# Eight more rows of the second batch's first stage computed before the steady loop, the last reads of the first batch's way back on other queues, and the first token group's sums by halves

## The chip, the cores and the metric

The kernel runs on one core of a Trainium2 chip. A core has a TensorE for matrix products (PE), a VectorE (DVE), a ScalarE (ACT), a GpSimd (POOL) and a SyncE (SP) that issues transfers; transfers run on 16 DMA engines. Metric: the device time of one execution in microseconds (us), the median over the runs shown.

## The reference

Eight batches of 3008 tokens by 256 channels go through a Fourier filter along the tokens, and the result goes token by token through a two-layer network of 2048 hidden units:

```python
X = np.fft.rfft(x, axis=1)
Y = X * (filt_r + 1j * filt_i)[None]
y = np.fft.irfft(Y, n=x.shape[1], axis=1)
h = y.reshape(B * S, D) @ w_in
out = (h - np.tanh(h)) @ w_out
```

x and the filters are float32; the weights arrive as 64-bit floats and are turned into float32 on the chip.

## The kernel before

3008 tokens are taken as 64 times 47. The forward transform has a **first stage** (for each residue r of 0 to 23 one product of a 128-row factor with 128 rows of x, called "row r" here, result into the DRAM buffer `ct1[b]`), a **middle** (products over the residues, the filter, products back, result into `ct2[b]`), and a **last** stage that reads `ct2[b]` for a group of 4 residues and leaves the group's tokens, transposed, in the tile `ut`. Six groups of 448 or 512 tokens make a batch. Each group then goes through four units U of the network: `up` (x, y, z, o banks), `shrink` (h minus tanh h, on ACT and DVE), `down` (accumulates the output). A unit counter U runs over 192 units; unit U issues its `up`, the `shrink` of U - 1 and the `down` of U - 2, interleaved by hand (the schedule is manual: every engine's queue holds its instructions in the order in which the program issues them).

**The prologue** (pools `pro` and `ps0`) does the whole transform of batch 0 up to `ct2[0]`, slot by slot: seven slots g, each with `across`, `there0`, `filtered` and a way back (`back0`, for the last slot `back`) whose results are copied by ACT to tiles e1 and stored into `ct2[0]` (trace name ct<-e). The stores of slots 0 to 2 are issued by POOL, 3 and 4 by SP, 5 by ACT, 6 half by ACT and half by SP. When slots 0 to 4 are stored, `rest(0, 25, ...)` (line 1129) reads 25 rows of each of four blocks into the tile `e2` of the first token group; when 5 and 6 are stored, a second `rest` reads the other 7 rows of each (trace name e<-ct). Both are four reads, issued by SP. Then SP issues the first loads of `first(2)` (see below), PE does rows 0 to 7 of batch 1 (`first1`, line 1227; four ACT copies, four stores on SP, line 1234) and 8 warming products (`warmer(8)`, line 1081) whose results are not used.

**Around it** the weights are converted from 64 bits by a chain of steps, one on ACT (line 181) and six or seven on DVE (lines 183 to 201), and combined by sums on DVE (lines 229, 232, 238). `convert(100)` issues what is left of the first five conversion jobs; the other eleven (`late`) are spread over the units U up to 5 by `converting(n)`. Their raw data is loaded by POOL (line 175).

**Then** `last(0)` (line 595 on PE, tile pu) makes the first group's tokens: 64 small products into two banks, "even" and "odd", an ACT copy of odd (line 601), a DVE sum and a DVE difference (lines 605, 606) into `ut`. Four further warming products (line 1374) fill PE until `ut` is there, and U = 0 starts (line 719, tile x).

**First stages in the loop.** `first(2, z2, [(1, c) for c in range(2, NX)])` is a generator of ten steps: rows 8 to 23 of batch 1 (four steps of four rows) and all of batch 2 (six). A step (lines 308 to 313, trace name pf) is four products into two banks, two ACT copies into the one tile a1, and a store by ACT. The list `due` says at which position 20c + 5u + k (group c, unit u of the group, place k of 0 to 4 in the unit) the next step is issued: ten positions from 4 on, 3 apart.

Of the kernel before, what the change touches and what calls it, by code (L numbers as in the profile page):

```python
# [9 lines left out]
F32 = mybir.dt.float32  # L10
# [11 lines left out]
SG = 5  # L22
# [95 lines left out]
def kernel(  # L118
# [27 lines left out]
    def dram(t, off, dims):  # L146
        return bass.AP(tensor=t, offset=off, ap=[list(d) for d in dims])
# [112 lines left out]
            for u in dict(after).get(k, ()):  # L260
                yield from sums(u)

    def load_x(t, b, r, n):

        nc.sync.dma_start(t[0:64, 0:n, :], dram(x.tensor, (b * SEQ + r) * DM,
                                                [[NR * DM, 64], [1, n * DM]]))
        lo = 1 if r == 0 else 0
        if lo:
            nc.sync.dma_start(t[64:128, 0, :], dram(x.tensor, b * SEQ * DM,
                                                    [[NR * DM, 64], [1, DM]]))  # L270
        nc.sync.dma_start(t[64:128, lo:n, :], dram(x.tensor, (b * SEQ + NR - r - lo) * DM,
                                                   [[NR * DM, 64], [-DM, n - lo], [1, DM]]))
        return t

    rows = slice(0, 64), slice(64, 128)
# [302 lines left out]
    def widths(c):  # L578

        return [128 if r else 64 for r in order(c)]  # L580
# [3 lines left out]
    def last(i, z, held=False):  # L584

        b, c = groups[i]
        n = sum(widths(c))
        e2, gt = e2s.pop(i)
        ut = dn.tile([128, 2, CH * 128], F32, tag="ut", bufs=2, name="ut")
        banks = z("pu", [128, 2, CH, 64])  # L590
        for h in range(2):
            for j, r in enumerate(order(c)):
                for bank, half in zip(banks, rows):
                    for m, part in enumerate(rows):
                        nc.tensor.matmul(bank[part, h, j],  # L595
                                         e2[half, r - CH * c, h * 128 + 64 * m:h * 128 + 64 * m + 64],
                                         gt[half, r - CH * c], start=True, stop=True)
        even, odd = banks
        for k in (1, 0) if held else (1,):
            t = tr.tile([128, 2, CH, 64], F32, tag="e1", bufs=2, name=("even", "odd")[k])  # L600
            ACT.copy(t, banks[k])
            even, odd = (even, t) if k else (t, odd)
        u4 = ut.rearrange("p h (j n) -> p h j n", n=128)
        m = sum(w == 128 for w in widths(c))
        V.tensor_add(u4[:, :, :, 0:64], even, odd)
        V.tensor_sub(u4[:, :, 0:m, 127:63:-1], even[:, :, 0:m], odd[:, :, 0:m])
        w = n // 2
        if i == 0:
            uts[i] = (ut, None, w)
            yield  # L610
            return
# [420 lines left out]
    with tc.tile_pool(name="tr", bufs=2) as tr, tc.manual_schedule():  # L1032
# [16 lines left out]
        with tc.tile_pool(name="pro", bufs=1) as pro, \  # L1049
# [169 lines left out]

            first0(2)  # L1220

            def first1(x1):

                for r in range(0, 8, 2):
                    pf = z0("pf", [128, 2, DM])
                    for k in range(2):
                        nc.tensor.matmul(pf[:, k], f0[:, r + k], x1[:, r + k],
                                         start=True, stop=True)
# [4 lines left out]
                    ACT.copy(a1, pf)  # L1233
                    nc.sync.dma_start(
                        dram(ct1[1], r * DM, [[NH * DM, 128], [1, 2 * DM]]), a1)
                    yield

            a2 = {0: across(0)}
            convert(5)
# [19 lines left out]
            for g in range(last_g + 1):  # L1259
                if g == 2:  # L1260
                    x1 = load_x(big([128, 8, DM], F32, "x1"), 1, 0, 8)
                if g + 2 <= last_g:
                    a2[g + 2] = across(g + 2)
                    if g + 2 < last_g:
                        fts[g + 2] = filters_of(g + 2)
                        if g == 1:
                            fts[last_g] = filters_of(last_g)
                    else:
                        turned_in(fts[last_g])
                if g == 3:  # L1270
# [37 lines left out]
            next(late)  # L1308
            warmer(8)

        with tc.tile_pool(name="dn", bufs=2) as dn, \
                tc.tile_pool(name="ps", bufs=1, space=bass.MemoryType.PSUM) as ps:
# [57 lines left out]
            for _ in last(0, z2):  # L1370
                pass
            warm = psl([128, 256], "o3")
            for _ in range(4):
                nc.tensor.matmul(warm[0:KM], mats[:, 3 * KM:4 * KM], mats[:, 3 * KM:3 * KM + 256],
                                 start=True, stop=True)
# [147 lines left out]
```

## Time and profile before

| what | us |
|---|---|
| median of 3 runs | 2543.22 (2541.65 to 2544.98) |
| profiled execution, its time | 2542.18 |
| profiled execution, its span | 2540.3 |
| PE busy | 2522.6 |
| DVE busy | 1935.6 |
| the first token group's products (pu) start | 76.05 |
| U = 0 starts | 79.77 |

A row of the timeline is: start in us from the span's start, length in us, engine, line, operation, written tile, read tiles, shapes and count, and in brackets how long the engine had been idle and what ended that. A fp32 product counts twice in the rows. SPq, ACTq and POOL rows with DMA_DIRECT2D are the issues of transfers. In the chain of waits a row is start, length, and what the time went to. A row of the stretches is the stretch, its length, busy time and count of PE, PEld, DVE, ACT, POOL, the granted clock, the DMA share and GB/s.

### The profile page before, as it was taken

Reading aid. Unit: us, or ns where it says so; the run is one execution under the profiler, and the core shown is the slowest. Engines: PE = TensorE matmul, PEld = TensorE weight load, DVE = VectorE, ACT = ScalarE, POOL = GpSimd, SP = SyncE. Lnnn points to the kernel's source line nnn. Section 1 sums busy time; section 2 is a strip of 40 time slices with the busy share of each in tenths; the row PEclk is TensorE's granted clock in tenths of the full one; section 3 lists DMA queues with packets and bytes.
Section 4 is the critical chain, followed back from the end, with each engine's and each line's share of the span. In section 5 each row is a group of like instructions: output and inputs, shape, how many; then the busy total and the mean of one; then the engine's idle time right before and its main releaser. Section 6 shows DMA issues by size and latency. Waiting matters only on the chain.

```text
span 2540.3 us, 44575 instructions
## 1 busy us (share of the span) xinstructions
PE 2522.6 (99%) x17072; PEld 2173.1 (86%) x17072; DVE 1935.6 (76%) x2270; ACT 1694.2 (67%) x2551; POOL 1532.0 (60%) x1112
## 2 busy tenths in 40 slices
PE   9999999999999999999999999999999999999998
PEld 8678889888898888988888888898889888898887
DVE  6888877988678876888669886698866888555555
ACT  4666666667666766676667666666666666666665
POOL 5255665667556765676656665666655666455552
PEclk9999999999999999999999999999999999999999
DMA  9854224422343323342334322343123322110110
GB/s 245 261 150 117 65 54 100 112 65 53 86 108 91 82 69 89 80 112 59 80 87 105 87 56 72 96 111 89 36 72 84 92 66 53 26 31 19 25 22 19
DMA packets 333664, 211.37 MB, mean 83 GB/s; under 512 B 231645, under 2 KB 305531, under 8 KB 329793
## 3 DMA queue, kind: packets, MB, share of 16 engines
q1 hardware_dynamic: 319091, 184.93, 29.8%
q0 software_dynamic: 11120, 16.16, 2.3%
q10 hardware_dynamic: 3230, 7.34, 0.9%
q8 instruction: 136, 2.23, 0.4%
q14 instruction: 87, 0.71, 0.1%
HBM read 127.81 MB, written 83.39 MB: 83 GB/s over the span
## 4 chain that ended last, share of the span: by engine, by line
PE 96%; DVE 2%; DMA 1%; issue 0%; POOL 0%; ACT 0%; ACTq 0%; SPq 0%; POOLq 0%; DVEq 0%
PE o L821 44%; PE x L648 25%; PE z L648 12%; PE y L648 6%; PE pm L415 2%; PE pu L595 2%; PE pm L351 1%; PE o L883 1%; PE pf L308 1%; DMA filt<-in_filt_r_dram 1%; DMA x<-in_x_dram 0%; DMA ct<-e 0%; PE o L719 0%; PE x L719 0%; PE z L719 0%
## 5 line engine op out<-in xcount | busy, mean ns | idle before, releaser
L821 PE MATMUL o<-t,wd 128*128 128x256 f32 (+1 forms) x3008 | 762.7, 376 | 0.0
L619 POOL TENSOR_TENSOR t<-h 128x512 f32<-128x512 f32 (+1 forms) x184 | 303.6, 1650 | 707.3 <-DVE h L771 642.2
L771 DVE TENSOR_TENSOR h<-h,y 128x1024 f32<-128x1024 f32 (+1 forms) x384 | 571.0, 1487 | 156.4 <-ACT y L767 156.4
L821 PEld LDWEIGHTS o<-t,wd 128*128 128x128 f32 x3008 | 568.8, 190 | 84.5 <-POOL o L853 15.1
L648 PE MATMUL x<-tu,wu 128*128 128x256 f32 (+1 forms) x2256 | 571.4, 376 | 0.0
L821 PE MATMUL o<-h,wd 128*128 128x256 f32 (+1 forms) x2256 | 569.9, 375 | 0.2 <-DVE h L771 0.2
L648 PEld LDWEIGHTS x<-tu,wu 128*128 128x128 f32 x2256 | 427.4, 190 | 53.8 <-issue 3.9
L821 PEld LDWEIGHTS o<-h,wd 128*128 128x128 f32 x2256 | 428.3, 190 | 50.9 <-issue 0.8
L654 ACT COPY s<-x 128x512 f32<-128x512 f32 (+1 forms) x188 | 109.3, 581 | 517.4 <-PE x L648 517.3
L764 ACT ACTIVATE y<-y 128x1024 f32<-128x1024 f32 (+1 forms) x384 | 399.5, 1040 | 12.1
L767 ACT ACTIVATE y<-y 128x1024 f32<-128x1024 f32 (+1 forms) x384 | 399.8, 1041 | 4.6
L761 ACT ACTIVATE y<-h 128x1024 f32<-128x1024 f32 (+1 forms) x384 | 400.6, 1043 | 2.5 <-DVE h L697 1.7
L622 POOL TENSOR_TENSOR t<-h,t 128x512 f32<-128x512 f32 (+1 forms) x184 | 338.3, 1838 | 0.0
L620 POOL TENSOR_TENSOR t<-h,t 128x512 f32<-128x512 f32 (+1 forms) x184 | 310.5, 1688 | 14.4
L621 POOL TENSOR_TENSOR t<-h 128x512 f32<-128x512 f32 (+1 forms) x184 | 276.9, 1505 | 0.0
L654 ACT COPY u<-x 128x512 f32<-128x512 f32 (+1 forms) x376 | 214.1, 569 | 72.9 <-PE x L648 69.6
L697 DVE COPY h<-x 128x512 f32<-128x512 f32 (+1 forms) x188 | 127.6, 679 | 129.1 <-PE x L648 128.9
L689 DVE TENSOR_TENSOR h<-z,u 128x512 f32<-128x512 f32 (+1 forms) x188 | 127.2, 677 | 88.9 <-ACT u L654 88.5
L648 PE MATMUL x<-ut,wu 128*128 128x256 f32 (+1 forms) x752 | 194.0, 380 | 0.2 <-DVE h L697 0.2
L648 PE MATMUL z<-tu,wu 128*128 128x256 f32 (+1 forms) x752 | 190.2, 375 | 1.4 <-DVE h L705 1.4
L648 PE MATMUL y<-ut,wu 128*128 128x256 f32 (+1 forms) x752 | 190.1, 375 | 0.0
L648 PE MATMUL z<-ut,wu 128*128 128x256 f32 (+1 forms) x752 | 190.0, 375 | 0.0
(215 smaller groups left out, 2933.5 us busy)
## 6 DMA issues: line engine op xcount, KB each, us to landing
ft<-filt SPq DMA_DIRECT2D x28, 1024.0 KB
ct<-nn SPq DMA_DIRECT2D x56, 512.0 KB
e<-ct SPq DMA_DIRECT2D x47, 512.0 KB
a<-ct SPq DMA_DIRECT2D x112, 192.0 KB
out_dram<-ot SPq DMA_DIRECT2D x1248, 16.0 KB
x_sb<-in_x_dram SPq DMA_DIRECT2D x110, 128.0 KB
ct<-a SPq DMA_DIRECT2D x60, 128.0 KB
ct<-x_sb SPq DMA_DIRECT2D x60, 128.0 KB
```

The source lines that it names most:

```text
L619: by.tensor_sub(t[0], b[0][1], b[0][0])
L620: by.tensor_sub(t[1], b[1][1], t[0])
L621: by.tensor_sub(t[2], b[1][1], b[0][1])
L622: by.tensor_sub(t[3], b[1][0], t[1])
L648: nc.tensor.matmul(bank[:, k], wu[:, q - 1, (2 * u + k) * 128:(2 * u + k + 1) * 128], rhs[q - 1], start=(first and k == 0), stop=True, ski ...
L654: ACT.copy(t, X)
L697: V.tensor_copy(h[:, 2, :, 0:w], X)
L761: ACT.activation(y[k], ht[k], AF.Arctan, scale=TURN)
L764: ACT.activation(y[k], y[k], AF.Tanh, scale=BEND)
L767: ACT.activation(y[k], y[k], AF.Square, scale=SCALE, accum_out=y_sums[:, 2 * U + k // 2:2 * U + k // 2 + 1])
L771: V.tensor_mul(ht[k], ht[k], y[k])
L821: nc.tensor.matmul(product(q), wd[:, q - 1, (2 * u + k) * 128: (2 * u + k + 1) * 128], rhs[q - 1][:, k], start=(u == 0 and k == 0 and q == ...
```

## The change

- `load_x` takes a queue. In slot 5 of the prologue POOL issues two more loads: rows 8 to 15 of batch 1 (`x1b`, 1 MB in all), ahead of two raw weight loads.
- The first `rest` (25 rows) is issued by POOL instead of SP. The second is issued alternately by SP and ACT.
- `convert(100)` and rows 0 to 7 (`first1(x1, 0, ...)`) now stand ahead of the second `rest`; rows 8 to 15 (`first1(x1b, 8, ...)`) behind it. `first1` is an ordinary function now; its stores are issued by POOL, two of 4 KB a partition instead of four of 2 KB, for each eight rows. The tiles of rows 8 to 15 are two of the `raw` buffers.
- `warmer(8)` becomes `warmer(2)`, the four warming products after pu become two.
- `first(2, ...)` has eight steps instead of ten, and `due` eight positions from 4 on, 3.75 apart.
- For the first token group the copy, the sum and the difference of `last` are made for each half of the channels.

```diff
-    def load_x(t, b, r, n):
+    def load_x(t, b, r, n, queue=nc.sync):
...
+        if i == 0:
+            t = tr.tile([128, 2, CH, 64], F32, tag="e1", bufs=2, name="odd")
+            for h in range(2):
+                ACT.copy(t[:, h], odd[:, h])
+                V.tensor_add(u4[:, h, :, 0:64], even[:, h], t[:, h])
+                V.tensor_sub(u4[:, h, 0:m, 127:63:-1], even[:, h, 0:m], t[:, h, 0:m])
+            uts[i] = (ut, None, n // 2)
+            yield
+            return
...
-            def first1(x1):
-
-                for r in range(0, 8, 2):
+            def first1(x1, at, tiles):
+
+                for r in range(at, at + 8, 2):
...
                     if r % 4 == 0:
-                        two = (tr.tile([128, 2, 2, DM], F32, tag="a1", bufs=1, name="a1") if r else
-                               buffer("xy").rearrange("p (m n) c -> p m n c", m=2))
-                    a1 = two[:, r // 2 % 2]
-                    ACT.copy(a1, pf)
-                    nc.sync.dma_start(
-                        dram(ct1[1], r * DM, [[NH * DM, 128], [1, 2 * DM]]), a1)
-                    yield
+                        two = tiles.pop(0)()
+                    ACT.copy(two[:, r // 2 % 2], pf)
+                    if r % 4:
+                        G.dma_start(dram(ct1[1], (r - 2) * DM, [[NH * DM, 128], [1, 4 * DM]]),
+                                    two.rearrange("p m n c -> p (m n c)"))
...
                 if g == last_g - 1:
+                    x1b = load_x(big([128, 8, DM], F32, "x1b"), 1, 8, 8, G)
                     ahead += [begun(tiles1, job, queue=G) for job in jobs[7:9]]
...
-            rest(0, SG * (last_g - 1), [nc.sync])
+            rest(0, SG * (last_g - 1), [G])
             way_back()
-            rest(SG * (last_g - 1), NA - SG * (last_g - 1), [nc.sync])
-            fs = first(2, z2, [(1, c) for c in range(2, NX)])
+            convert(100)
+            first1(x1, 0, [lambda: buffer("xy").rearrange("p (m n) c -> p m n c", m=2),
+                           lambda: tr.tile([128, 2, 2, DM], F32, tag="a1", bufs=1, name="a1")])
+            rest(SG * (last_g - 1), NA - SG * (last_g - 1), [nc.sync, ACT])
+            fs = first(2, z2, [(1, c) for c in range(4, NX)])
             next(fs)
-            convert(100)
-            for _ in first1(x1):
-                pass
+            first1(x1b, 8, [raw_tile, raw_tile])
...
-            warmer(8)
+            warmer(2)
...
-            for _ in range(4):
+            for _ in range(2):
                 nc.tensor.matmul(warm[0:KM], mats[:, 3 * KM:4 * KM], mats[:, 3 * KM:3 * KM + 256],
...
-            due = [4 + (LEAD - 4) * k / (NX + 4) for k in range(NX + 4)]
+            due = [4 + (LEAD - 4) * k / (NX + 2) for k in range(NX + 2)]
```

More of the change, by code (lines that the diff above doesn't have):

```diff
@@ L261, in weights @@
                 yield from sums(u)
-    def load_x(t, b, r, n):
-        nc.sync.dma_start(t[0:64, 0:n, :], dram(x.tensor, (b * SEQ + r) * DM,
-                                                [[NR * DM, 64], [1, n * DM]]))
+    def load_x(t, b, r, n, queue=nc.sync):
+        queue.dma_start(t[0:64, 0:n, :], dram(x.tensor, (b * SEQ + r) * DM,
+                                              [[NR * DM, 64], [1, n * DM]]))
         lo = 1 if r == 0 else 0
         if lo:
[L269 to L272, printed above, removed]
+            queue.dma_start(t[64:128, 0, :], dram(x.tensor, b * SEQ * DM,
+                                                  [[NR * DM, 64], [1, DM]]))
+        queue.dma_start(t[64:128, lo:n, :], dram(x.tensor, (b * SEQ + NR - r - lo) * DM,
+                                                 [[NR * DM, 64], [-DM, n - lo], [1, DM]]))
         return t
@@ L598, in last @@
         even, odd = banks
+        u4 = ut.rearrange("p h (j n) -> p h j n", n=128)
+        m = sum(w == 128 for w in widths(c))
+        if i == 0:
[7 more added lines that the diff above has]
+            return
         for k in (1, 0) if held else (1,):
@@ L602, in last @@
             even, odd = (even, t) if k else (t, odd)
-        u4 = ut.rearrange("p h (j n) -> p h j n", n=128)
-        m = sum(w == 128 for w in widths(c))
         V.tensor_add(u4[:, :, :, 0:64], even, odd)
@@ L607, in last @@
         w = n // 2
-        if i == 0:
-            uts[i] = (ut, None, w)
-            yield
-            return
         tu = dn.tile([128, 4, 256], F32, tag="tu", bufs=2, name="tu")
@@ L1220, with raw_tile @@
             first0(2)
-            def first1(x1):
-                for r in range(0, 8, 2):
+            def first1(x1, at, tiles):
+                for r in range(at, at + 8, 2):
                     pf = z0("pf", [128, 2, DM])
                     for k in range(2):
-                        nc.tensor.matmul(pf[:, k], f0[:, r + k], x1[:, r + k],
+                        nc.tensor.matmul(pf[:, k], f0[:, r + k], x1[:, r + k - at],
                                          start=True, stop=True)
                     if r % 4 == 0:
-                        two = (tr.tile([128, 2, 2, DM], F32, tag="a1", bufs=1, name="a1") if r else
-                               buffer("xy").rearrange("p (m n) c -> p m n c", m=2))
-                    a1 = two[:, r // 2 % 2]
-                    ACT.copy(a1, pf)
-                    nc.sync.dma_start(
-                        dram(ct1[1], r * DM, [[NH * DM, 128], [1, 2 * DM]]), a1)
-                    yield
+                        two = tiles.pop(0)()
[3 more added lines that the diff above has]
+                                    two.rearrange("p m n c -> p (m n c)"))
+            def raw_tile():
+                t = pro.tile([128, 512], I64, tag="raw", bufs=3, name="a1")
+                return t.bitcast(F32).rearrange("p (m n c) -> p m n c", m=2, n=2)
             a2 = {0: across(0)}
```

## The prediction

> **What bounds the kernel now.** I read the page first, then busy time by stretches, the chain of waits, and the timelines of PE, SP, ACT, POOL and DVE between 50 and 145 us. The page's first part says that PE is nearly always busy. The chain holds the only hole that the edits touch:
>
> ```profile
> PE 2522.6 (99%) x17072; PEld 2173.1 (86%) x17072; DVE 1935.6 (76%) x2270; ACT 1694.2 (67%) x2551; POOL 1532.0 (60%) x1112
> ```
>
> ```profile
> 58.74 7.30 DMA ct<-e
> 66.12 0.59 ACT e L1144
> ...
> 69.65 3.61 DMA ct<-e
> 73.68 2.23 DMA e<-ct
> 76.71 1.15 PE pu L595 x60
> ...
> 106.26 1.73 PE pf L308 x8
> ...
> 141.14 0.61 DVE h L697
> ```
>
> ```profile
> 66.55 3.62 PE L1227 MATMUL pf<-x,f 128*128 128x256 f32 x16
> 70.00 3.62 PE L1081 MATMUL warm<-f 128*128 128x256 f32 x16
> 76.05 0.33 PE L595 MATMUL pu<-gt,e 64*64 64x64 f32 x4 [2.42 <-DMA e<-ct]
> ...
> 77.79 1.99 PE L1374 MATMUL pt<-mats_sb 120*120 120x256 f32 x8
> 79.77 1.77 PE L719 MATMUL x<-ut,wu 128*128 128x448 f32 x4
> ...
> 141.79 1.13 PE L648 MATMUL x<-ut,wu 128*128 128x256 f32 x4 [0.17 <-DVE h L697]
> ```
>
> From 70.00 to 76.05 PE does nothing useful: 3.62 us of warming and 2.42 of waiting for the last reads, which waited for the stores before them (3.61, then 2.23). So 3.5 us of real products fit there free. But the chain leaves PE again later: at 141.79 PE waits for DVE. The wait is only 0.17 us, because PE itself was busy up to there; the stretches tell how near DVE is to its limit:
>
> ```profile
> 60.00:66.00 6.00, 6.00 (x31) 5.11 (x30) 4.32 (x11) 1.76 (x3) 0.21 (x1) 1.00 0.97 353
> 66.00:70.00 4.00, 4.00 (x23) 3.59 (x22) 3.76 (x9) 2.12 (x5) 0.00 (x0) 1.00 0.65 183
> 70.00:74.00 4.00, 3.62 (x17) 2.85 (x15) 3.83 (x7) 1.83 (x4) 0.00 (x0) 1.00 0.29 96
> ...
> 100.00:120.00 20.00, 20.00 (x61) 11.21 (x59) 18.98 (x38) 15.59 (x25) 8.18 (x13) 1.00 0.97 297
> 120.00:142.00 22.00, 21.84 (x138) 14.75 (x138) 21.20 (x44) 13.07 (x21) 10.47 (x12) 1.00 0.82 233
> ```
>
> The third busy figure is DVE's: 18.98 of 20 us, then 21.20 of 22. From U = 1 to U = 5 PE and DVE, which converts weights, are both full. Work taken from PE alone is no time there.
>
> **The change part by part.** *The last reads.* SP's rows, and the wait that the waits of SP name:
>
> ```profile
> 66.57 1.75 SPq L1129 DMA_DIRECT2D e<-ct  x4
> 69.65 0.82 SPq L483 DMA_DIRECT2D ct<-e  x2
> ...
> 73.28 1.36 SPq L1129 DMA_DIRECT2D e<-ct  x4
> ```
>
> ```profile
> SPq L483 <- DMA e<-ct: 1.3, 1, 1.3
> ```
>
> SP issues the 25-row reads at 66.57, and its halves of slot 6's stores stand behind them; they left at 69.65 after a wait of 1.3 us for a landing of these reads, though ACT had copied their data earlier. With the 25-row reads on POOL, SP's stores leave with ACT's copies. The last reads need those stores, and two of the four now also need ACT to be free:
>
> ```profile
> 67.12 0.37 ACT L481 COPY e<-pe 112x256 f32<-112x256 f32 x1 [0.41 <-PE pe L478]
> ...
> 70.74 1.09 ACT L1233 COPY a<-pf 128x512 f32<-128x512 f32 x2
> 77.94 0.59 ACT L601 COPY odd<-pu 128x512 f32<-128x512 f32 x1 [6.11 <-PE pu L595]
> ...
> 82.96 0.67 ACT L181 ACTIVATE xy<-ft 128x512 f32<-128x512 f32 x1 [3.86 <-DMA ct<-xy]
> ...
> 101.08 1.07 ACT L310 COPY a<-pf 128x512 f32<-128x512 f32 x2 [2.06 <-DMA ct<-a]
> ```
>
> ACT finishes the copies of rows 0 to 7 at 70.74 + 1.09 = 71.83. Its two reads take 1.36 / 4 = 0.34 us each, the second leaves at about 72.2 and lands 2.23 us later, at 74.4. Before, the last one landed just ahead of 76.71. That is a gain of 2.3 us if nothing else moves. Behind ACT's reads stand the four copies of rows 8 to 15 (about 2.1 us) and the copy of odd; ACT sat idle 6.11 us there, so they are covered; without that cover, or if pu has to wait for a bank that they free, they cost up to 2.1.
>
> *The added load* of 1 MB goes out at about 56 us. DMA was 0.97 busy at 353 GB/s in 60:66, so it adds 3.0 us of transfer to that stretch. POOL's issue:
>
> ```profile
> 1.29 3.29 POOL L1184 DMA_DIRECT2D x<-in_x_dram  x5 [0.83 <-POOLq L1507]
> ...
> 59.48 0.72 POOL L175 DMA_DIRECT2D a<-in_moe_w_in_dram  x1 [2.54 <-ACT xy L432]
> ```
>
> Two issues at 3.29 / 5 = 0.66 us make 1.3, inside POOL's idle 2.54; the four stores and four reads that POOL also gets fall into 60 to 80, where it does nearly nothing (0.21, 0.00, 0.00 us above). The two raw loads behind the new one land some 3 us later and are read after 82.96: covered. The transfer is not free: ACT's copy at 66.12 waited for a store that took 7.30 us under this load, and everything of ACT above follows it. Between 0 and 3.0 us of delay I take 0.7, nearer to zero, because the load stands in POOL's queue between raw weight loads that kept the engines as full up to 66 anyway; what it does is to hold them full some 3 us longer. So pu's main part starts at 75.1 instead of 76.71: **gain 1.6**, ends 2.3 and 2.3 - 3.0 = -0.7.
>
> *PE in the hole.* Rows 0 to 7 to 70.0, rows 8 to 15 another 3.45 (66.55 to 70.00), two warming products 3.62 / 4 = 0.9: PE is free at 74.4, before 75.1. Cost nothing; without the wait for the reads as cover, 3.45 - 6 x 0.45 = 0.75. The loads for `first(2)`, on SP behind two reads instead of four, move forward with them: nothing. Two fewer warming products behind pu: nothing, they only fill the wait for `ut`.
>
> *The halves.* From the end of pu (77.86) PE waited until 79.77, 1.9 us, for copy, sum and difference. Half a copy is 0.37 (the 112x256 row), half a sum and half a difference some 0.4 each by the 0.69 of the whole: PE can start 1.2 after pu, 0.65 earlier. DVE does four instructions instead of two and is done no earlier: for DVE, nothing, between -0.3 and +0.2.
>
> *Two steps fewer in the loop.* Positions were 4, 7, 10, ... 31, now 4, 7.75, 11.5, 15.25, 19, 22.75, 26.5, 30.25. From U = 4 on a step goes only to place 2 of a unit, so what disappears is one step in U = 2 (the 106.26 row, 1.73 us) and that of U = 4: 3.46 us of PE, all ahead of 141.79. With the halves PE would come 4.1 us earlier to U = 5 than DVE's start of `ut` alone allows. DVE has the same list of work, so PE then waits for DVE's copy L697, which frees the bank x. What counts is how much idle time DVE loses:
>
> ```profile
> 75.28 0.69 DVE L201 TENSOR_TENSOR wu<-top,low 128x512 f32<-128x512 f32 x1
> 78.56 0.69 DVE L605 TENSOR_TENSOR ut<-pu,odd 128x512 f32<-128x512 f32 x1 [2.58 <-DMA x_sb<-in_x_dram]
> ...
> 83.67 0.43 DVE L183 TENSOR_SCALAR xy<-xy 128x512 f32<-128x512 f32 x1 [0.52 <-ACT xy L181]
> ...
> 92.93 1.09 DVE L771 TENSOR_TENSOR h<-h,y 128x896 f32<-128x896 f32 x1 [0.69 <-ACT y L767]
> ...
> 97.15 0.43 DVE L183 TENSOR_SCALAR xy<-xy 128x512 f32<-128x512 f32 x1 [0.61 <-ACT xy L181]
> ...
> 106.03 1.09 DVE L771 TENSOR_TENSOR h<-h,y 128x896 f32<-128x896 f32 x1 [0.37 <-ACT y L767]
> ```
>
> The idle 2.58 ahead of `ut` is the hole itself; up to 75.97 DVE still converts, so `ut` can move by 2.5 at most. Of the other 2.19 us (0.52 + 0.69 + 0.61 + 0.37): the 0.52 goes, since ACT had waited 3.86 us for a store of rows 0 to 7 that SP issued late and POOL issues some 5 us earlier; the 0.37 goes, since ACT had waited 2.06 us for the tile a1 of steps that now stand further apart; of the 0.61, where ACT's step stood behind the copies of a pf step, half; the 0.69, ACT's own three activations in a row, stays. **Gain 1.2**, ends 0 and 2.2.
>
> *The sum:* 1.6 + 1.2 = 2.8 us. The profiled execution's span 2540.3 would be 2537.5, its time 2542.18 would be 2539.4; it lies 1.0 under the median of 2543.22, so the median becomes 2540.4, 0.11% less. A measurement here can tell about 0.2%, 5.1 us, from no change.
>
> On the stores: one took 3.61 us while the engines were only 0.65 and 0.29 busy, the later read 2.23. The Trainium skill, page "DMA: Bandwidth & Descriptors", section "Why a DMA increments its semaphore by 16 and not by 1", says that a transfer issued by SP or ACT uses the largest number of engines up to 16 that divides its slowest dimension, so 25 rows would crowd onto five; the half-idle engines agree with it. By that rule the stores land in some 2.2 us once those reads are on another queue, and the sum would be the 2.3 end, 3.5 in all; by the rows alone it is 2.8.
>
> **The rivals.** *DVE does not hold PE back*: its 2.19 us and the small gaps close as PE runs ahead, and PE's whole relief counts: 1.6 + 0.65 + 3.46 = 5.7, median 2537.5. For it speaks PE's 99%; against it the DVE figures of 100:142. *The reads do not come earlier*: the stores stay as slow under the added load, and the first term is 0: gain 1.2, median 2542.0. For it speaks the 7.30 store. *Slower*: the 25-row reads, now behind the x load and two raw loads in POOL's queue, land last. Loads issued by POOL took up to this:
>
> ```profile
> x<-in_x_dram POOLq DMA_DIRECT2D x5, 256.0 KB, 10.6
> raws<-in_moe_w_in_dram POOLq DMA_DIRECT2D x2, 512.0 KB, 6.5
> ```
>
> Four issues of 0.7 from 67 on leave the last at 69.1 to 69.8; landing 10.6 later, at 80.2, pu is 3.5 late, and after the 1.2 from DVE the kernel is 2.3 slower, 2545.5. It decides from a landing at 77.9 on (76.7 + 1.2). Against it: raw loads of twice the size landed in 6.5 us (the last figure of a row is from issue to landing), and DMA is 0.29 busy at 70:74. The same page, section "Queues, rings and completion order", has a queue's transfers consumed in ring order on each engine, which is this mechanism; no run here shows it yet.
>
> **How the numbers follow.** Forecast 0.55 (own range 2538.7 to 2541.5), reads unmoved 0.2, PE's whole relief 0.13, slower 0.12. The range 2536.9 to 2544.8 takes in the second and third whole and the near part of the last. Beyond 5.1 us faster lies most of the third case: 0.12. Beyond 5.1 us slower lies a landing past 83: 0.05. The rest, 0.83, is within 0.2%.
>
> **What would show it.** SP's two ct<-e issued right after ACT's copies, the first near 67.6 instead of 69.65; the last e<-ct issue on ACT near 73; pu's long row near 75.1; one PE wait of 2 to 3 us on DVE between 130 and 140, where 0.17 stood; the DVE idle at 83.67 and 106.03 gone; from U = 5 on everything shifted by one amount. I am wrong if PE has no such wait (the whole relief), if ACT's reads leave after 74, or if pu waits for reads that POOL issued.

## The result, and the profile after

The changed kernel takes 2558.57 us (median of 4 runs, 2557.36 to 2563.49) against 2542.43 us for the kernel before in the same comparison: a ratio of 1.0066, 95% interval 1.0054 to 1.0079. It is 16.1 us slower; forecast was 2540.4, 2.8 us faster. The profiled execution took 2563.49, the longest of the four; its span is 2561.6 us, 21.3 more than before's 2540.3.

The timeline of PE in the changed kernel (start, duration, line, tiles, count; in brackets the idle time ahead and what ended it). L478 (unmoved) holds the last slot's products on the way back, with 1.04 us before; L1232 the rows of the second batch, L724 and L653 the up products, five lines further down than before.

```profile
75.30 2.02 PE L478 MATMUL pe<-xy,mats_sb 112*112 112x128 f32 x8 [8.24 <-DVE xy L458]
77.11 4.85 PE L1232 MATMUL pf<-x,f 128*128 128x256 f32 x16
81.79 3.62 PE L1232 MATMUL pf<-x1b,f 128*128 128x256 f32 x16
...
88.91 1.91 PE L595 MATMUL pu<-gt,e 64*64 64x64 f32 x64 [2.64 <-DMA f<-f_both]
...
97.94 3.35 PE L724 MATMUL x<-ut,wu 128*128 128x448 f32 x4 [5.13 <-DVE ut L606]
...
159.43 1.13 PE L653 MATMUL z<-ut,wu 128*128 128x256 f32 x4 [1.22 <-DVE h L694]
161.16 1.77 PE L653 MATMUL x<-ut,wu 128*128 128x256 f32 x4 [0.60 <-DVE h L702]
```

The whole loss can be placed with these rows and those of before. The products of rows 0 to 7 start at 77.11 instead of 66.55: 10.6 us late. From there to pu it is 11.8 us instead of 9.5 (88.91 - 77.11; 76.05 - 66.55): 2.3 more. From pu to U = 0 it is 9.0 instead of 3.7 (97.94 - 88.91; 79.77 - 76.05): 5.3 more. U = 0 is 18.2 us late, and U = 5, at 161.16 instead of 141.79, is 19.4 late. The last 1.9 us of the 21.3 are lost behind it. So three places are to be explained: ahead of L478, ahead of pu, ahead of `ut`. The 2.3 ahead of pu are mostly rows 0 to 7, which take 4.85 us for 3.62, and the two warming products that are left (1.03); the wait itself, 2.64 for 2.42, has hardly grown. (The view puts it down to the load of f, but pu reads only gt and e.)

*Ahead of L478* two waits end nearly together. PE's own is for DVE, which filters slot 6; DVE's timeline in the changed kernel:

```profile
72.29 0.69 DVE L447 TENSOR_TENSOR nn<-xy,filt_end 112x512 f32<-112x512 f32 x1 [10.13 <-DMA ct<-e]
```

The view names a store, but the row reads only xy and filt_end. With the load alone added to the kernel before (below), the view of DVE's waits names slot 6's filter (filt_end), whose last pieces SP issues as loads of 24 KB; before, this wait was 1.5:

```profile
DVE nn L447 <- DMA filt_end<-filt: 8.7, 1, 8.7
```

The chain of waits of the changed kernel goes by the other wait, ACT's for a tile that a store of slot 3 still reads:

```profile
58.92 16.23 DMA ct<-e
...
75.25 0.59 ACT e L1149
```

A store of slot 3 took 16.23 us where one had taken 7.30. So PE got its operands at 75.1, and ACT could copy at 75.25: both small transfers are late. The view of DMA issues (KB each, median us from issue to landing), first of the kernel before between 50 and 76 us, then of the changed kernel:

```profile
a<-in_moe_w_out_dram POOLq DMA_DIRECT2D x1, 512.0 KB, 7.3
a<-in_moe_w_in_dram POOLq DMA_DIRECT2D x1, 512.0 KB, 6.4
```

```profile
x1b<-in_x_dram POOLq DMA_DIRECT2D x2, 512.0 KB, 12.3
...
a<-in_moe_w_out_dram POOLq DMA_DIRECT2D x1, 512.0 KB, 14.6
a<-in_moe_w_in_dram POOLq DMA_DIRECT2D x1, 512.0 KB, 14.3
```

The two raw loads and the store that share these microseconds with the added load take twice as long. The stretches of the changed kernel (busy time of PE, PEld, DVE, ACT and POOL, then PE's clock, the share of the DMA engines and GB/s) show that the engines are full and yet move less:

```profile
60.00:66.00 6.00, 6.00 (x30) 5.11 (x29) 2.08 (x5) 1.96 (x4) 0.73 (x1) 1.00 1.04 246
66.00:70.00 4.00, 1.06 (x5) 0.55 (x4) 0.00 (x0) 0.00 (x0) 0.00 (x0) 0.92 1.03 285
70.00:74.00 4.00, 0.00 (x0) 0.00 (x0) 1.65 (x4) 0.00 (x0) 0.00 (x0) 0.50 0.66 225
...
90.00:100.00 10.00, 4.87 (x35) 2.92 (x30) 2.74 (x7) 1.76 (x4) 0.00 (x0) 0.50 0.69 242
```

In 60:66 before, 0.97 busy gave 353 GB/s; now 1.04 gives 246. The granted clock falls to 0.50 in and behind each long hole; L478 takes 2.02 us for 1.04 before, the products of rows 0 to 7 take 4.85 for 3.62, U = 0's first four 3.35 for 1.77.

*Ahead of `ut`*, POOL's two stores of rows 8 to 15 and DVE's sum in the changed kernel:

```profile
86.22 0.53 POOL L1238 DMA_DIRECT2D ct<-a  x1 [2.81 <-ACT a L1236]
87.20 0.53 POOL L1238 DMA_DIRECT2D ct<-a  x1 [0.45 <-ACT a L1236]
```

```profile
97.20 0.42 DVE L605 TENSOR_TENSOR ut<-pu,odd 128x256 f32<-128x256 f32 x1 [11.33 <-DMA f<-f_both]
```

The tiles of these stores are raw tiles of the prologue's pool, which is closed right behind them. `ut` is the first tile that is taken from the next pool, in the same memory. The view names the load of f as what ended the wait, but nothing in `ut` is computed from f; it only landed near the end of it. The second store took 9.4 us to land, so it ended near 96.6. Whether the closed pool is what DVE waits for is for an experiment to say.

### The profile page after: what moved, and what is told of

Its sections match the earlier page's. It is cut to its first block, busy times and chain, and to the rows that moved or that the text cites. A ratio compares the mean times of both kernels' runs of the same rounds, so it can differ in the third digit from the quotient of the medians.

```text
span 2561.6 us, 44536 instructions
## 1 busy us (share of the span) xinstructions
PE 2528.3 (99%) x17056; PEld 2175.4 (85%) x17056; DVE 1936.2 (76%) x2272; ACT 1694.4 (66%) x2552; POOL 1537.8 (60%) x1122
## 3 DMA queue, kind: packets, MB, share of 16 engines
q8 instruction: 136, 2.23, 0.3%
## 4 chain that ended last, share of the span: by engine, by line
PE 93%; DMA 3%; DVE 2%; POOL 0%; issue 0%; ACT 0%; SPq 0%; ACTq 0%; POOLq 0%; DVEq 0%
PE o L826 44%; PE x L653 25%; PE z L653 12%; PE y L653 6%; PE pm L415 2%; PE pu L595 2%; DMA ct<-e 1%; PE pm L351 1%; DMA f<-f_both 1%; DMA x<-in_x_dram 1%; DVE h L776 0%; DMA filt<-in_filt_r_dram 0%; PE pf L308 0%; PE o L888 0%; DVE xy L194 0%
## 5 line engine op out<-in xcount | busy, mean ns | idle before, releaser
L653 PE MATMUL x<-tu,wu 128*128 128x256 f32 (+1 forms) x2256 | 571.4, 376 | 0.0
L653 PEld LDWEIGHTS x<-tu,wu 128*128 128x128 f32 x2256 | 427.4, 190 | 54.1 <-issue 4.2
L653 PE MATMUL x<-ut,wu 128*128 128x256 f32 (+1 forms) x752 | 194.6, 381 | 0.6 <-DVE h L702 0.6
L653 PE MATMUL z<-tu,wu 128*128 128x256 f32 (+1 forms) x752 | 190.2, 375 | 1.4 <-DVE h L710 1.4
L653 PE MATMUL z<-ut,wu 128*128 128x256 f32 (+1 forms) x752 | 190.1, 375 | 1.2 <-DVE h L694 1.2
L653 PE MATMUL y<-ut,wu 128*128 128x256 f32 (+1 forms) x752 | 191.0, 377 | 0.0
```

The source lines that it names most:

```text
L653: nc.tensor.matmul(bank[:, k], wu[:, q - 1, (2 * u + k) * 128:(2 * u + k + 1) * 128], rhs[q - 1], start=(first and k == 0), stop=True, ski ...
```

## The experiments

Each difference below is the median against the kernel before's median in the same comparison, with the ratio and its 95% interval.

**Load and tiles, each alone and both.** Of the changed kernel the load is left out, or the tiles of rows 8 to 15 are others (the free buffer of `xy` and the free slot of `e2`, which live on), or both.

```
e1, e5  -   x1b = load_x(big([128, 8, DM], F32, "x1b"), 1, 8, 8, G)
        +   first1(x1, 8, ...)          # rows 0 to 7 of x1 in their place
e2, e5  -   first1(x1b, 8, [raw_tile, raw_tile])
        +   first1(x1b, 8, [xy_tile, e2_tile])
```

> The changed kernel without the added 1 MB load: rows 8 to 15 are computed from the tile of rows 0 to 7, so these rows of batch 1 come out with wrong values; all instructions but the two loads stay. Load theory (the load in POOL's queue holds up SP's small transfers, and with them slot 6's filter): PE's wait of 8.24 us at 75.30 is gone, U = 0 starts 8 to 10 us earlier than at 97.94, the median falls from 2558.6 to about 2549. Store theory alone (only the stores of rows 8 to 15 cost): that wait stays, 2558. Reads theory (the reads that POOL and ACT issue are late by themselves): the wait at 75.30 has nothing to do with them, so it stays as well, and U = 0 starts as late.

> The changed kernel with rows 8 to 15 copied to two tiles of the pool that outlives the prologue (the second xy buffer and the free e2 tile) instead of two raw tiles of the prologue's own pool. Store theory (the first writes into the next pool wait until POOL's two stores out of the old pool have landed): the 5.13 us of PE's wait for ut and the 11.33 us of DVE's idle time ahead of it go, U = 0 starts about 5 us earlier, with the clock regained 6 to 7, median about 2552. Load theory alone: within 1 us of 2558.6. Reads theory: pu itself is what is late, so the wait for ut moves by less than 1 us.

> Of the changed kernel, the added load of x1b is left out (rows 8 to 15 are computed from the rows of x1, so their values are wrong) and their two output tiles come from buffers that live on (the other xy buffer and the free e2 slot) instead of the pool that closes. If the load and the hand-over of the closed pool's memory are the two main costs, both waits of PE go: under 1.5 us ahead of L478, no wait over 2 us for ut, pu's long row near 77.5 as in the run without the load, U = 0 within 1 us of the kernel before's 79.77, time 2541 to 2545. If the two costs only hide a third one (the last reads landing late among the other transfers), the wait for e<-ct ahead of pu stays at 2 us or more and U = 0 starts at 82 or later, time 2546 to 2549.

Measured: without the load +5.5 us (1.0019, 1.0009 to 1.0028); with the other tiles +6.5 (1.0025, 1.0014 to 1.0036); with both +0.5 (1.0003, 0.9994 to 1.0013). Timelines of PE, of the run without the load, of that with the other tiles, and of that with both:

```profile
66.38 1.10 PE L478 MATMUL pe<-xy,mats_sb 112*112 112x128 f32 x8 [0.84 <-DVE xy L458]
...
85.19 3.35 PE L724 MATMUL x<-ut,wu 128*128 128x448 f32 x4 [5.53 <-DVE ut L606]
```

```profile
68.22 1.10 PE L478 MATMUL pe<-xy,mats_sb 112*112 112x128 f32 x8 [1.20 <-DVE xy L458]
...
83.35 0.48 PE L595 MATMUL pu<-gt,e 64*64 64x64 f32 x4 [5.32 <-DMA f<-f_both]
85.12 1.97 PE L595 MATMUL pu<-gt,e 64*64 64x64 f32 x60 [1.30 <-DMA e<-ct]
```

```profile
77.02 0.33 PE L595 MATMUL pu<-gt,e 64*64 64x64 f32 x4 [2.04 <-DMA e<-ct]
78.07 1.29 PE L595 MATMUL pu<-gt,e 64*64 64x64 f32 x60 [0.72 <-DMA e<-ct]
```

The wait for `ut` (5.53) stays without the load and goes with the other tiles: it is the stores out of the closed pool. In the next pair of runs, the chain of the one with the raw tiles (e3) names such a store itself:

```profile
81.64 8.08 DMA ct<-a
...
90.29 0.42 DVE ut L605
```

Whether any last user of the pool makes `ut` wait, or only one whose bytes `ut` takes over, wasn't tried. The tiles are then worth 5.0 us without the load (5.5 - 0.5), the slow products behind the wait included. The wait ahead of L478 goes without the load. With the load and the other tiles that execution waits little at L478, but 6.6 us (5.32 + 1.30) ahead of pu: the load's cost has another place there, 6.0 us (6.5 - 0.5). In that execution slot 6's filter came in time, but slot 3's store took 11.44 us and held ACT's copies, and with them the last stores and reads: SP's first last read leaves at 78.99, against 71.59 without the load. Both together cost 15.6 (16.1 - 0.5), 4.6 more than the two alone. What makes the rest wasn't settled; the slow clock is a candidate, since with the holes filled, below, the changed kernel is at +10.7, about the 11.5 of the two costs alone.

**What it is about the load.** First, its order: x1b ahead of the two raw loads or in place of them, the raw loads then behind the 25-row reads; with the raw tiles (e3) and with the other tiles (e4).

```
-   ahead += [begun(tiles1, job, queue=G) for job in jobs[7:9]]      # at g == last_g - 1
    rest(0, SG * (last_g - 1), [G])
+   ahead += [begun(tiles1, job, queue=G) for job in jobs[7:9]]
```

> The changed kernel with the added load in the place of the two raw weight loads, which POOL issues after its 25-row reads instead: as many bytes in POOL's queue between 50 and 66 us as before the change. Load theory: what counts is the 1 MB on top of a full queue, so the result is that of the run without the load, about 2549, with the wait at 75.30 gone; the raw loads land about 80 and cost at most 1 us. If it is the form of the load (rows of 8 KB, and of 1 KB backwards) and not the amount, the wait stays above 4 us and the median near 2556.

> Both of the last two edits. Load and store theory together: U = 0 starts near 79 and the rest goes as the prediction had it, median 2540 to 2543, about as before the change. If a third cause of some size is there (the reads' queues, the halves, fewer warming products), 2545 or more.

Measured: +13.0 (1.0045, 1.0028 to 1.0061) and +6.3 (1.0022, 1.0013 to 1.0032), against +16.1 and +6.5 with the load in addition. To hold the bytes of that stretch nearly equal gives back 3.1 us with the raw tiles, where the intervals overlap, and nothing that can be told with the others. L478 still waited 3.91 us with the raw tiles and 4.99 with the others, and there pu another 4.85 (4.20 + 0.65). So the bare number of bytes is not the whole cause: the stretch 60:66 moves 242 GB/s at 1.02 in e4, with the added load in the place of two raw loads of the same size. By the sign named beforehand this points to the form of the load; but the raw loads, moved back, now also run beside the last stores and reads, so it isn't shown.

Next, the load alone, added to the kernel before and read by nothing: on POOL at the changed kernel's place, on SP at that place, half of it on POOL, and on POOL some 12 us earlier, behind the load of x1.

```
+   load_x(big([128, 8, DM], F32, "x1b"), 1, 8, 8, G)        # e10; nc.sync: e11; 4 rows: e14
    ahead += [begun(tiles1, job, queue=G) for job in jobs[7:9]]
...
    x1 = load_x(big([128, 8, DM], F32, "x1"), 1, 0, 8)
+   load_x(big([128, 8, DM], F32, "x1b"), 1, 8, 8, G)        # e15
```

> The kernel before with the added load of x1b alone, in POOL's queue at the place where the changed kernel has it; nothing reads it, and rows 8 to 15 stay in the loop. If the load by itself starves SP's small stores, ct<-e of slot 3 takes over 12 us instead of 7.30, PE waits 4 us or more ahead of its L481 where it waited for nothing, and the kernel is 4 to 8 us slower (2546.5 to 2550.5). If it costs its 3 us of transfer at most, as the prediction had it, L481 waits under 3 us and the kernel is 0 to 3 us slower; by the value the prediction took, 0.7 us slower.

> As the run before it in this call, but the same dead load is in SP's queue, at the same place in the program. If only the amount counts (1 MB, 3.0 us at 353 GB/s), the kernel is slower by the same as with the load on POOL, within 1.5 us. If what hurts is a second queue of large packets that takes turns with SP's small ones, SP's small stores now stand behind the load in one queue and are late by its 3 us at most: PE waits 3 us or less ahead of L481 and the kernel is at least 2 us faster than with the load on POOL.

> The kernel before with the dead load on POOL at the changed kernel's place, of half the size (four rows, 0.5 MB); nothing reads it. If the cost goes with the bytes that the full engines have to move, it is half of the 8.1 us of the whole load, 3 to 5 us: time 2545.5 to 2548, wait ahead of L478 2.5 to 4.5. If there is slack for the first bytes (the prediction's 0.7 for a load of 1 MB, or a threshold), it costs under 1.5 us; if any load in that queue delays SP's stores by the same round, it costs 6 us or more.

> The kernel before with the whole dead load (1 MB, nothing reads it) on POOL at the early place, behind x1's, near 41 us instead of 57. If the place decides, it costs 0 to 2 us (2542.7 to 2544.7), with no wait over 1.5 us ahead of L478; if the prologue has no room for 1 MB anywhere, 5 us or more.

Measured: +8.1 on POOL (1.0033, 1.0020 to 1.0045), +7.1 on SP (1.0028, 1.0018 to 1.0038), +3.4 for the half (1.0015, 1.0005 to 1.0024), +5.7 early (1.0018, 1.0007 to 1.0029; its runs spread from 2541.78 to 2551.18). (Where an expectation says L481, the products are L478 in the rows.) PE's timelines of the four, in this order:

```profile
72.72 2.02 PE L478 MATMUL pe<-xy,mats_sb 112*112 112x128 f32 x8 [6.84 <-DVE xy L458]
```

```profile
82.95 0.48 PE L595 MATMUL pu<-gt,e 64*64 64x64 f32 x4 [8.22 <-DMA e<-ct]
```

```profile
79.28 0.48 PE L595 MATMUL pu<-gt,e 64*64 64x64 f32 x4 [5.62 <-DMA e<-ct]
```

```profile
61.52 0.78 PE L1139 MATMUL pe<-nn,mats_sb 120*120 120x256 f32 x2 [2.40 <-DVE nn L453]
```

My theory that large packets in POOL's queue starve SP's small ones fell: from SP's own queue the load costs as much, within 1.0 us. What the queue decides is the stage that is late. On POOL it is slot 6's filter and slot 3's store; on SP the filter comes in time and ACT's last copy of slot 5 is 2.9 us late (68.97 instead of 66.12), but slot 4's stores stand behind the load. By the chain of that run the second leaves at 63.82 and lands at 74.5; the 25-row reads wait for it, SP's half of slot 6's stores stands behind these, and pu waits 8.22.

```profile
63.82 10.72 DMA ct<-e
```

Half the load costs about half (3.4 of 8.1), though its wait stands ahead of pu and not, as expected, ahead of L478; so there is no sign of slack for the first bytes. The early place is not free either: the stretch from 40 to 50 us that looked free was 0.83 busy, the filters' loads that SP issues there for the next slots come late (the last from 55.21 instead of 50.67), and PE waits at 61.52 and again, 1.49 us, at 63.80. Whether 5.7 is less than 8.1 can't be told; the two intervals overlap. The stretch 60:66 with the load on POOL, then with the load on SP:

```profile
60.00:66.00 6.00, 5.88 (x28) 4.65 (x26) 0.95 (x3) 1.17 (x2) 0.26 (x1) 1.00 1.00 197
```

```profile
60.00:66.00 6.00, 5.56 (x26) 4.27 (x24) 5.62 (x11) 1.76 (x3) 0.00 (x0) 1.00 1.06 322
```

1 MB at 353 GB/s is 3.0 us; at the 197 of the run on POOL it is 5.3. But the run on SP moves 322 in the same stretch, and 200 only in the next, and costs about as much: the low rate of one stretch doesn't explain the cost by itself.

Then the late place, in the changed kernel with the other tiles: POOL issues the load behind the 25-row reads.

```
-   x1b = load_x(big([128, 8, DM], F32, "x1b"), 1, 8, 8, G)        # at g == last_g - 1
    rest(0, SG * (last_g - 1), [G])
+   x1b = load_x(big([128, 8, DM], F32, "x1b"), 1, 8, 8, G)
```

> The changed kernel, whole and with right values, with two edits: POOL issues the load of x1b after the 25-row reads (near 69) instead of ahead of the raw loads, when the transfers of 60 to 66 are through, and the tiles of rows 8 to 15 are such as live on. If the place of the load is what costs, PE's wait ahead of L478 is under 1.5 us, x1b lands near 73 to 75, rows 8 to 15 are done near 77.5 to 78.5 and pu follows, U = 0 at 80 to 82, and the time is 2543 to 2546. If the load costs its 6 to 7 us wherever it stands in the prologue (now by making the last reads late), the time is 2548.5 to 2550.5 as with the load at its first place.

Measured: +7.0 (1.0025, 1.0016 to 1.0035), as at its first place. L478 waits only 0.47 now, and the whole cost stands ahead of the products that need the load:

```profile
78.90 5.80 PE L1232 MATMUL pf<-x1b,f 128*128 128x256 f32 x16 [8.35 <-DMA x1b<-in_x_dram]
```

**The last reads.** Without the load and with the other tiles, as above, and all four last reads on SP.

```
-   rest(SG * (last_g - 1), NA - SG * (last_g - 1), [nc.sync, ACT])
+   rest(SG * (last_g - 1), NA - SG * (last_g - 1), [nc.sync])
```

> As the run before it in this call (no load of x1b, wrong values in rows 8 to 15, tiles that live on), and the four last reads all on SP as in the kernel before, so that the loads of the first(2) steps stand behind all four of them and not beside ACT's two. If those loads are what makes the reads land late, the last e<-ct lands 1 to 3 us earlier and pu starts at 75.0 to 76.5; time 1 to 3 us under the run before it. If the stores of rows 0 to 7 that POOL issues make them late, or nothing does, pu starts within 0.5 us of the run before it or up to 0.7 us later (two more issues of 0.34 us on SP).

Measured: -1.2 us (0.9996, 0.9987 to 1.0006), 1.6 under the run with two queues; the two intervals overlap. The timelines of PE: with ACT's two reads pu's long row starts at 78.07 (above); with all on SP:

```profile
77.34 1.15 PE L595 MATMUL pu<-gt,e 64*64 64x64 f32 x60 [0.50 <-DMA e<-ct]
...
79.72 1.77 PE L724 MATMUL x<-ut,wu 128*128 128x448 f32 x4 [0.17 <-DVE ut L606]
...
138.76 1.13 PE L653 MATMUL z<-ut,wu 128*128 128x256 f32 x4 [1.49 <-DVE h L694]
140.49 1.97 PE L653 MATMUL x<-ut,wu 128*128 128x256 f32 x4 [0.60 <-DVE h L702]
```

pu comes 0.7 us earlier although SP issued its first last read 1.1 us later (72.69 instead of 71.59). The chain of the run with two queues says why:

```profile
72.84 4.98 DMA e<-ct
78.07 1.29 PE pu L595 x60
```

ACT's read left at 72.84 and took 4.98 us where 2.23 had stood, with the loads of the next steps from SP and the stores of rows 0 to 7 from POOL beside it. In this pair of traces the second queue is a loss, and its company is the likely reason; the medians alone don't show it, and which of the two transfers counts most wasn't separated.

**PE's relief alone.** The kernel before without the products and copies of two pf steps; x itself is stored for rows 8 to 15, and every transfer stays.

```
    for m, bank in enumerate(banks):
+       if b == 1 and c < 4:
+           a1 = xt.rearrange("p (m n) c -> p m n c", m=2)
+           continue
```

> The kernel before, with the products and the ACT copies of two of the ten pf steps of the loop left out (rows 8 to 15 of the second batch; x itself is stored in their place, so the output is wrong): PE's relief of 3.46 us alone, with every transfer kept. If DVE bounds U = 1 to 5, PE's freed time turns into waits for DVE ahead of U = 5, U = 5 starts 0 to 1.2 us earlier than 141.79, and the kernel is 0 to 1.2 us faster (2542.2 to 2543.4 beside 2543.4). If PE's relief counts, U = 5 starts 3.4 us earlier, near 138.3, and the kernel is 3.4 us faster (2540.0).

Measured: -2.1 us (0.9993, 0.9984 to 1.0003). U = 5 in PE's timeline:

```profile
140.22 1.13 PE L651 MATMUL x<-ut,wu 128*128 128x256 f32 x4 [0.60 <-DVE h L700]
```

1.57 us earlier than 141.79, of 3.46 that PE was spared, and with a longer wait for DVE. But this execution reached its `ut` 0.5 us later than before's 78.56, as DVE's timeline has it:

```profile
79.06 0.69 DVE L608 TENSOR_TENSOR ut<-pu,odd 128x512 f32<-128x512 f32 x1 [1.84 <-ACT odd L604]
```

From there to U = 5 it takes 61.2 us instead of 63.2: 2.1 less, about the 1.8 of DVE's idle time that are gone (only 0.61 is left up to U = 5, where 2.41 had stood: the prediction's 2.19 and 0.22 at 122.17). Counted from U = 0, which stood 1.5 us later than before's (81.23), it is 3.0 less, near PE's whole relief. What tells the two apart is that PE still waits 0.60 for DVE, which itself is hardly idle: DVE is the bound there, by little. The time, -2.1, lies between the two expectations and doesn't decide between them.

**The 25-row reads on POOL and the halves alone.** The kernel before with these two parts; rows 8 to 15 stay in the loop.

```
-   rest(0, SG * (last_g - 1), [nc.sync])
+   rest(0, SG * (last_g - 1), [G])
    # and the loop over halves in the first token group's sums, as in the change
```

> The kernel before, with two parts of the change alone: the 25-row reads on POOL's queue, and the first token group's sums by halves; rows 8 to 15 stay in the loop, the last reads stay on SP. If term 1 of the prediction is right once nothing else crowds the queues, SP's slot-6 stores leave near 67.6 and 68.4 instead of 69.65, the last reads land near 74, pu's long row starts at 74 to 75.3, U = 0 1.5 to 2.5 us earlier than 79.77, and all of it lasts to the end: 2541 to 2542 beside 2543.4. If DVE's list of work holds U = 5 where it was, U = 0 moves but U = 5 stays within 0.5 us of 141.79, and the time is the same.

Measured: -1.1 us (0.9996, 0.9987 to 1.0006). SP's timeline, then PE's:

```profile
67.75 1.70 SPq L483 DMA_DIRECT2D ct<-e  x2
71.76 1.97 SPq L1134 DMA_DIRECT2D e<-ct  x4
```

```profile
75.67 1.15 PE L595 MATMUL pu<-gt,e 64*64 64x64 f32 x60 [0.60 <-DMA e<-ct]
...
78.58 1.67 PE L724 MATMUL x<-ut,wu 128*128 128x448 f32 x4
...
140.96 1.13 PE L653 MATMUL x<-ut,wu 128*128 128x256 f32 x4 [0.60 <-DVE h L702]
```

The stores leave 1.9 us earlier, the reads 1.5, pu 1.0, U = 0 1.2, U = 5 0.8: less at pu and U = 0 than expected, and U = 5 moves.

**The clock.** The changed kernel with PE kept busy in its two holes.

```
    rest(0, SG * (last_g - 1), [G])
+   warmer(14)
...
-   for _ in range(2):
+   for _ in range(8):                     # warming products ahead of U = 0
```

> The changed kernel with 14 more warming products ahead of L478 (14 x 0.45 = 6.3 us, inside the wait of 8.24) and eight instead of two ahead of U = 0; everything else as it is. If the halved clock after the long waits is a cost of its own, the granted clock of 74:80 and 90:100 goes back to near 1.00, L478 takes 1.10 instead of 2.02 and the products of rows 8 to 15 run at full speed, and the time falls by 2 to 4 us, to 2554.5 to 2556.5. If what follows waits for transfers anyway, U = 0 stays within 0.5 us of 97.94 and the time at 2557.5 to 2559.

Measured: +10.7 us (1.0047, 1.0030 to 1.0064), against +16.1: more than the 2 to 4 us that were expected, but the two intervals still overlap (1.0054 to 1.0064). PE's timeline:

```profile
71.49 1.04 PE L478 MATMUL pe<-xy,mats_sb 112*112 112x128 f32 x8
72.37 3.62 PE L1232 MATMUL pf<-x,f 128*128 128x256 f32 x16
...
92.07 1.77 PE L724 MATMUL x<-ut,wu 128*128 128x448 f32 x4 [1.62 <-DVE ut L606]
```

The products run at full speed again, and from L478 to U = 0 it is 20.6 us instead of 22.6. These 2.1 are about what L478 and rows 0 to 7 gain by the clock alone (2.02 - 1.04 and 4.85 - 3.62). From U = 0 to U = 5 (152.19) it is 60.1 instead of 63.2, another 3.1, of which U = 0's first four products are 1.6. That makes some 5 us in this pair of traces. L478's start 3.8 earlier is no gain of the warming, which moves no transfer ahead of it: here the filter came in time, L478 stood behind the warming products, and slot 3's store took 13.22 us instead of 16.23. So the clock is seen at work in the rows, and its share in the medians isn't shown.

**The whole change, mended.** All of the change, with the load at the early place, the other tiles, and the last reads on SP.

```
    x1 = load_x(big([128, 8, DM], F32, "x1"), 1, 0, 8)
+   x1b = load_x(big([128, 8, DM], F32, "x1b"), 1, 8, 8, G)
...
+   first1(x1b, 8, [xy_tile, e2_tile])
+   rest(SG * (last_g - 1), NA - SG * (last_g - 1), [nc.sync])
```

> The whole change with right values, mended at three places: POOL issues the load of x1b right behind that of x1, some 15 us earlier, where the transfers are 0.80 to 0.83 busy; the tiles of rows 8 to 15 live on past the closed pool; the four last reads all go on SP. If the load costs only because of where it stands, this is the run without a load and with all reads on SP (2541.5): U = 0 near 79.7, U = 5 near 140.5, time 2540.5 to 2543, 0 to 2 us under the kernel before. If the load costs wherever it stands in the prologue, some stage before 66 is late by 3 us or more, and the time is 2546 to 2550.

Measured: +3.0 us (1.0012, 1.0003 to 1.0020). It takes back 13 of the 16 us, but not the last three: against the run without the load and with the reads on SP (-1.2) the load still costs 4.2. No kernel that was tried and computes all of it beats the kernel before by more than a measurement can tell; the nearest is that of the reads and the halves alone.

## Why the prediction was wrong

- **The added load: the step that failed first.** "Between 0 and 3.0 us of delay I take 0.7": measured 8.1 alone and 6.0 inside the change. Both the value and the upper end were wrong. The end came from the rate before (353 GB/s), as if the load could add its bytes without making the other transfers slower; slot 6's filter, the stores of slots 3 and 4 and the raw loads all took longer, and on POOL the stretch 60:66 gave 197 to 246 GB/s with the engines full. Why it costs more than its bytes stays open: on SP the stretch gave 322, at about the same cost, and with raw loads moved away in exchange it hardly fell. And the reason for taking 0.7, that the engines were full there anyway, speaks for the opposite: a full resource on which the chain already waited (7.30 us for a store of 240 KB) leaves no cover for an added load.
- **Stores of rows 8 to 15, counted at nothing: the second.** The prediction priced POOL's issues (right: POOL did sit idle) and not whose memory the stores read. They were the last users of the closed pool, `ut` the first of the next, and PE lost 5.13 us there, 5.53 without the load; 5.0 us of the time in the runs without it.
- **"PE is free at 74.4, before 75.1"** assumed that x1b is there and the clock is 1.00. With the load late the clock fell to 0.50 behind the hole. The prediction had the two warming rows in hand and costed fewer of them at nothing.
- **The last reads, term 1 (gain 1.6, which is 2.3 less 0.7 for the load).** The first half of the mechanism is right: SP's stores left with ACT's copies (67.75). Measured without the load and with the reads on SP, the gain is 1.0 us at pu and 0.8 at U = 5, where 2.3 would have stood. The step that failed is when the last reads can leave. The term took them to leave when ACT is free, the last at 72.2, and left out that the last store comes behind ACT's second copy and has to land first: by the chain it left at 69.13 and took 3.60 us, as before's 3.61, and the last read left at 73.44. By the rule of the Trainium skill that the prediction weighed (page "DMA: Bandwidth & Descriptors", section "Why a DMA increments its semaphore by 16 and not by 1") it had the stores land in some 2.2; here the reads moved to another queue but still ran at the same time, from 67.52 on, so the run doesn't contradict the page, only the use made of it. ACT's two reads left near the time forecast (72.84 in the run with two queues), but took 4.98 us to land instead of 2.23.

```profile
69.13 3.60 DMA ct<-e
...
73.44 2.10 DMA e<-ct
```

- **DVE as the bound of the loop, term 2 (gain 1.2): the mechanism held.** In the run without the load and with the reads on SP the loop from U = 0 to U = 5 takes 60.8 us (140.49 - 79.72) instead of 62.0: 1.2 less, with PE waits of 1.49 and 0.60 for DVE in the place of 0.17, as forecast for 130 to 140. That it is the 1.2 forecast is in part luck. The term counted DVE's idle time, and from the start of `ut` (78.98) to U = 5 it is 61.5 instead of 63.2, 1.7 less: the 0.61, of which the forecast let half go, went whole, and so did 0.22 at 122.17 that it didn't count, beside the 0.52 at 83.67 and the 0.37 at 106.03. The only idle time of DVE that is left in the loop up to U = 5 is the one that was to stay, below. The halves did what was forecast: U = 0 stands 1.2 us behind the end of pu there (79.72; 78.49), before 1.9.

```profile
92.87 1.09 DVE L776 TENSOR_TENSOR h<-h,y 128x896 f32<-128x896 f32 x1 [0.68 <-ACT y L772]
```

PE's relief alone gave 2.1 of 3.46 counted from `ut`, over the 1.2 and inside the end of 2.2. The rival "PE's whole relief" fell with the waits of 1.49 and 0.60, which together with the 1.2 are about PE's 3.46; so did the slower rival's mechanism (25-row reads late on POOL); a slower kernel came about in another way.
- **The chances** gave 0.05 to slower by over 5.1 us. All the ways to it that were priced led through one late read; a load of 1 MB into a stretch at 0.97 should have been a rival of its own, with the ends 3.0 and, by the 7.30 us that 240 KB took there, far beyond.

## What to carry to other kernels

Before a transfer is moved, ask what the chain waits for in the stretch where it will run. Here 1 MB cost 5.7 to 8.1 us in stretches that were 0.83 and 0.97 busy, on either of two queues, and 6.5 (7.0 - 0.5) at a later place, where the products that need it waited instead; none of the places tried was free. The free time of PE is no reason to move work to a place whose data must come over a full resource. When the last users of a pool are moved, ask which first tile of the next pool lies behind them. Work that fills a hole of one engine pays only what the next bound, here DVE, leaves of it, so price the receiving bound before the move.

## What was not expected of the hardware

With the added load on POOL the engines moved fewer bytes in the same busy time: 246 and 197 GB/s at 1.04 and 1.00 in 60:66, against 353 at 0.97. A full share has no one rate, though: on SP the same load gave 322 at 1.06 there, and the kernel before moves 297 at 0.97 in 100:120. What makes the bytes slower (the form of the load, rows in reversed order in its second half, or the mixture with small stores) wasn't separated; the runs with raw loads moved away in exchange point to the form. The granted clock halved inside a hole of PE of 8.24 us (0.50 in 70:74 of the changed kernel) and around one of 5.13 us (0.50 in 90:100), and the products right behind ran at half speed: 2.02 us for 1.04, 3.35 for 1.77. Runs with the early load spread over 9.4 us (2541.78 to 2551.18) where the kernel before spreads over 5.2 in that comparison (2540.28 to 2545.52).
